# A state-space scan and two MLPs on one core: another order of the units and spread decays in the opening

## Chip, cores, metric

The kernel runs on one core of a Trainium2 chip. The metric is the device time of one execution in microseconds; lower is better. Before the change it is 644.33 us, the median of three runs (644.09 to 645.01).

## What is computed

Four batches of eight heads, 768 positions, head size 32, state size 16. A scan with decays `a` gives y, its 3072 rows of 256 go through an MLP with an ELU (256 to 2048 to 256) and then through a gated one (256 to 1536 to 256).

```python
for c in range(nc):                          # chunks of a sequence
    cum = cumsum(log(clip(a, 1e-6, 1))[c])
    L = exp(cum[i] - cum[j]) * (i >= j)
    y = ((C @ B.T) * L) @ x + (C @ state) * exp(cum)
    state = exp(sum(la)) * state + sum_j B[j] * x[j] * exp(cum[-1] - cum[j])
h = x @ w_in
x = where(h > 0, h, exp(min(h, 0)) - 1) @ w_out
out = (silu(x @ w_gate) * (x @ w_val)) @ w_out2
```

## The kernel before

The scan is cut into 24 units of 128 positions of one batch (all heads at once). Unit t belongs to batch t // 6, chunk t % 6, so four consecutive units mostly follow each other in one sequence. The first eight units (`CUT`) are handled as two halves of 64 positions (`R`) each. The tokens go through MLP 1 in six blocks of 512, four units a block.

Steps of a unit: E (L316), a scan on VectorE that turns the decays, broadcast by DMA to all partitions (`abc`), into the products of decays; P (L334), the running products per head (from `ahn`); cb (L375, TensorE) is B times C; m (L381) multiplies E by cb; bn and ct (L354, L346, GpSimd) weight B by the last column of E and C by P; u (L392, TensorE) is the unit's contribution to the state; sc (L403, L405, VectorE) steps the state; sb (L417, GpSimd) spreads it into block-diagonal form for y (L451 for the part from the state, L458 for the inner part); out (L474, ScalarE) and xl (L478, VectorE) split y into high and low parts xh and xl, the input of MLP 1. Later units do the same with other shapes (L442, L446, L370, L340). The state lies in two buffers `sc` that units use in turn: a unit reads one and writes the other.

MLP 1 runs in slots, one hidden tile f of 128 a slot: h (L493, six matmuls), ScalarE's relu and exp (L515, L520), VectorE's L521, c (L535 in block 0, L542 later). h has two PSUM banks, so h(i+2) waits for L521 of slot i. Weights come packed; tile f is decoded by ScalarE (ex, L137) and three steps on VectorE (L140, L143, L147), then split by ScalarE (wh, L179) and GpSimd (wl, L183). In block 0 each slot decodes the weight of three slots later, with the steps of units 4 to 7 among it.

Before the slots stands the opening: units 0 to 3 and the first weights. Every engine runs its instructions in the order in which they are written, and for the opening that order is written out by hand in `ORDER`, one word a step: `Labc0` loads abc of unit 0, `cl` clips it, `d10 d00 d20` are the decode steps of weight 0, `acl aclip acs` load all of `a`, clip it and write it to DRAM (`ac`), from where all units but the first two read their decays. `first.close()` then gives the PSUM banks of `cb_odd` and `y_odd` to h and c. All loads are issued by SyncE's queue (SP) in that same order. After the opening, `OFF`, `OFF1`, `OFF8` give for each step of a unit the slot and the place in it (early, mid, late).

Of the kernel before, what the change touches and what calls it, by code (L numbers as in the profile page):

```python
# [18 lines left out]
Q = 128  # L19
R = 64  # L20
# [38 lines left out]
ORDER = """Labc0 Lbc0 ident cl0 mz0 ident8 Labc1 cb0 Lahn0 LW0 E0 Lbc1 cl1 mz1 Lx0 Lahn1 ex0 d10 d00 P0 acl d20 E1 cb1 Lx1 blk
bn0 m0 wh0 Lbc2 aclip LW1 ct0 u0 wl0 acs P1 bn1 m1 sc0 sb0 ct1 ex1 u1 d01 y0 d11 Labc2 out0  # L60
LW2 Lahn2 xl0 Lx2 sc1 d21 sb1 wh1 y1 Labc3 wl1 mz2 E2 Lbc3 cb2 P2 out1 Lx3 bn2 xl1 Lahn3 ex2 ct2 m2 u2 LW3 d02 d12 d22 sc2 sb2
wh2 mz3 E3 cb3 y2 wl2 P3 bn3 out2 xl2 ct3 m3 u3 Labc4 Lbc4 Lx4 Lahn4 sc3 sb3 y3 out3 xl3 Labc5 Lbc5 Lx5 Lahn5""".split()

# [6 lines left out]
def ssm_mlp_glu_kernel(ctx, tc, a, bcs, xbc, w1, w2, consts, out):  # L70
# [41 lines left out]
    sbd = [ast.tile([128, 2, 128], F32, name=f"sbd{i}") for i in range(2)]  # L112
    sc = [ast.tile([128, 2, 2 * D], F32, name=f"sc{i}") for i in range(2)]

    ctz = [x2_all[:, 2 * NT - 2 * Q * (i + 1):2 * NT - 2 * Q * i].rearrange("p (g q) -> p g q", g=2) for i in range(2)]
    ident8_r = x2_all[:, 2 * NT - 4 * Q - H * R:2 * NT - 4 * Q]
    top = 2 * NT - 4 * Q - H * R - NT // 16

# [69 lines left out]
    an = BATCH * H * S // 128  # L188
    spare, at = {}, [0, 0]
    for t, tag, n in [(1, "bcraw", 1024), (2, "bcraw", 1024), (3, "bcraw", 1024), (1, "abc", 512), (2, "abc", 512),  # L190
                      (3, "abc", 512), (1, "xb", 512), (2, "xb", 512), (3, "xb", 512), (2, "E", 512),
                      (1, "ahn", 128), (2, "ahn", 128), (3, "ahn", 128)]:
        k = int(at[0] + n > top)
        spare[t, tag] = (x2_all, w2e)[k][:, at[k]:at[k] + n]
        at[k] += n

    for t, tag, i in [(5, "bcraw", 0), (6, "bcraw", 512), (7, "abc", 0), (4, "abc", 0)]:
        k = {5: 1, 6: 1, 7: 1, 4: 2}[t]
        spare[t, "xb"] = spare[k, tag][:, i:i + 512]
    acl = x2_all[:, top:top + an]  # L200
# [20 lines left out]
    def a_loads(t):  # L221
        b, c = divmod(t, NCH)
        u = U.setdefault(t, {})
# [96 lines left out]
    def q0(t):  # L320

        return 0 if t % NCH > 0 else R if t < CUT else Q

    def a_P(t):
        u = U[t]
        if q0(t) == Q:
            return
        z = u["ahn"][:, q0(t):]
        if t < DIRECT:
            nc.vector.tensor_scalar(z, z, 1.0, 1e-6, ALU.min, ALU.max)  # L330
        u["P"] = ap_.tile([128, Q], F32, tag="P", name="P")
# [89 lines left out]

    def a_sb(t):
        if t < CUT:
            spread(t, q0(t) // R, 2)
        if t + 1 >= CUT and t % NCH < NCH - 1:
            spread(t + 1, 0, 1)

    def a_state(t):
        a_sc(t)
        a_sb(t)  # L430
        if t >= CUT:
            U.pop(t)

    def a_y(t):


        u = U[t]
        has = t % NCH > 0
        if t >= CUT:
# [393 lines left out]
```

## Time and profile before

| | us |
|---|---|
| median of three runs | 644.33 |
| the profiled execution | 643.67 |
| its span, first to last instruction | 641.9 |
| TensorE busy | 616.2 |
| VectorE busy | 384.2 |
| ScalarE, GpSimd busy | 314.5, 315.5 |

The span is what the trace covers; the execution's own time is 1.8 us more. The engines run beside each other, so the busy times add up to far more than the span. In the rows below, a time that stands first is counted from the span's start.

### The profile page before, as it was taken

The page shows a single profiled execution, that of the slowest core. Times are in us where ns is not written, and L with a number is a line of the kernel's source. Part 1 is how long each engine was busy: PE and PEld are TensorE (multiplying, and loading weights), DVE is VectorE, ACT ScalarE, POOL GpSimd, SP SyncE. Part 2 cuts the span into 40 slices and gives each one's busy share as a digit, 9 for nine tenths or more (in the row PEclk, how much of TensorE's full clock was granted, in tenths as well). Part 3 has the DMA queues.
Part 4 walks back from the last instruction along what each step waited for, and adds up shares of the span by engine and source line. Part 5 has one row for each costly group of instructions (what it writes and reads, how often), then busy time and mean ns, then how long its engine had stood idle before and what let it go on. Part 6 is the DMA issues. An engine that isn't in the chain of part 4 may idle for free.

```text
span 641.9 us, 9664 instructions
## 1 busy us (share of the span) xinstructions
PE 616.2 (96%) x3620; PEld 490.1 (76%) x3620; DVE 384.2 (60%) x574; ACT 314.5 (49%) x568; POOL 315.5 (49%) x263
## 2 busy tenths in 40 slices
PE   2599999999999999999999999999999999999997
PEld 1456667888788878888888888888888888888886
DVE  5869987878887898783574663343343343343332
ACT  2156767667667766766775542322332232332322
POOL 3636756767878587874454333333333333333332
PEclk9999999999999999999999999999999999999999
DMA  6785534443543544400310000000000000000000
GB/s 184 203 287 193 168 117 145 138 146 128 144 143 132 152 133 132 135 34 18 98 51 0 2 2 0 34 0 1 33 1 1 33 1 0 34 0 2 33 1 33
DMA packets 21646, 49.54 MB, mean 77 GB/s; under 512 B 4320, under 2 KB 6496, under 8 KB 21600
## 3 DMA queue, kind: packets, MB, share of 16 engines
q1 hardware_dynamic: 21600, 48.93, 24.4%
q8 instruction: 28, 0.46, 0.3%
q14 instruction: 18, 0.15, 0.1%
HBM read 45.68 MB, written 3.24 MB: 76 GB/s over the span
## 4 chain that ended last, share of the span: by engine, by line
PE 94%; DVE 3%; issue 1%; SPq 1%; DMA 1%; ACT 0%; POOL 0%; POOLq 0%; DVEq 0%
PE h L493 21%; PE c L542 17%; PE o L493 15%; PE v L493 15%; PE g L493 15%; PE c L535 4%; PE cb L370 1%; PE y L446 1%; PE y L442 1%; DMA raw<-in_w 1%; DVE P L334 1%; DVE E L316 0%; DVE v L147 0%; PE y L392 0%; PE y L451 0%
## 5 line engine op out<-in xcount | busy, mean ns | idle before, releaser
L499 POOL TENSOR_TENSOR gl<-m,gh 128x512 fp32r<-128x512 f32 x152 | 200.2, 1320 | 249.1 <-ACT gh L498 244.0
L614 DVE TENSOR_TENSOR m<-m,g 128x512 f32<-128x512 f32 x72 | 49.5, 688 | 163.9 <-ACT m L609 163.9
L609 ACT ACTIVATE m<-g 128x512 f32<-128x512 f32 x72 | 43.0, 598 | 185.6 <-PE g L493 185.5
L521 DVE SCALAR_TENSOR_TENSOR m<-m,h 128x512 f32<-128x512 f32 x96 | 65.5, 682 | 59.2 <-ACT m L520 59.2
L498 ACT ACTIVATE gh<-m 128x512 fp32r<-128x512 f32 x152 | 94.8, 624 | 1.6 <-DVE m L615 1.0
L515 ACT ACTIVATE m<-h 128x512 f32<-128x512 f32 x96 | 56.8, 592 | 63.3 <-PE h L493 55.9
L493 PE MATMUL h<-xh,w1h 128*128 128x512 f32 x192 | 80.2, 418 | 1.6 <-DVE xl L478 1.1
L493 PE MATMUL h<-xh,w1l 128*128 128x512 f32 x192 | 75.6, 393 | 0.0
L542 PE MATMUL c<-gh,w1h 128*128 128x512 f32 x160 | 62.4, 390 | 0.0
L542 PE MATMUL c<-gh,w1l 128*128 128x512 f32 x160 | 62.3, 389 | 0.0
L520 ACT ACTIVATE m<-m 128x512 f32<-128x512 f32 x96 | 59.9, 624 | 0.5
L493 PE MATMUL h<-xl,w1h 128*128 128x512 f32 x192 | 59.8, 393 | 0.0
L493 PE MATMUL g<-x2h,w2h 128*128 128x512 f32 x144 | 56.0, 389 | 0.0
L493 PE MATMUL g<-x2h,w2l 128*128 128x512 f32 x144 | 56.0, 389 | 0.0
L493 PE MATMUL v<-x2h,w2h 128*128 128x512 f32 x144 | 56.0, 389 | 0.0
L493 PE MATMUL v<-x2h,w2l 128*128 128x512 f32 x144 | 56.0, 389 | 0.0
L493 PE MATMUL o<-gh,w2h 128*128 128x512 f32 x144 | 56.0, 389 | 0.0
L493 PE MATMUL o<-gh,w2l 128*128 128x512 f32 x144 | 56.0, 389 | 0.0
L493 PE MATMUL o<-gl,w2h 128*128 128x512 f32 x144 | 56.0, 389 | 0.0
L615 DVE TENSOR_TENSOR m<-m,v 128x512 f32<-128x512 f32 x72 | 49.5, 688 | 7.5
L542 PE MATMUL c<-gl,w1h 128*128 128x512 f32 x160 | 50.9, 389 | 0.0
L493 PEld LDWEIGHTS h<-xh,w1h 128*128 128x128 f32 x192 | 36.4, 189 | 14.0 <-DVE m L521 4.0
(125 smaller groups left out, 1089.4 us busy)
## 6 DMA issues: line engine op xcount, KB each, us to landing
abc<-ac SPq DMA_DIRECT2D x16, 512.0 KB
bcraw<-in_bcs SPq DMA_DIRECT2D x32, 256.0 KB
raw<-in_w SPq DMA_DIRECT2D x15, 512.0 KB
w2e<-in_w SPq DMA_DIRECT2D x12, 512.0 KB
xb<-in_xbc SPq DMA_DIRECT2D x17, 256.0 KB
raw<-in_w SPq DMA_DIRECT2D x12, 256.0 KB
out_y<-yo SPq DMA_DIRECT2D x12, 256.0 KB
abc<-ac SPq DMA_DIRECT2D x8, 128.0 KB
```

What stands on the lines that cost most here:

```text
L334: nc.vector.tensor_tensor_scan(u["P"][:, q:q + n], u["ahn"][:, q:q + n], zero_q[:, :n], 1.0, ALU.mult, ALU.add)
L493: nc.tensor.matmul(dst, lhsT=l, rhs=r, start=first and i == 0, stop=last and i == len(ops) - 1, **kw)
L498: nc.scalar.activation(hi, src, AF.Copy)
L499: lo_eng.tensor_tensor(lo, src, hi.bitcast(F32), ALU.subtract)
L515: nc.scalar.activation(m, h, AF.Relu, scale=-1.0)
L520: nc.scalar.activation(m, m, AF.Exp, scale=-1.0)
L521: nc.vector.scalar_tensor_tensor(m, m, -1.0, h, ALU.add, ALU.max)
L535: nc.tensor.matmul(cps[b][m], lhsT=W1["v", f][:, m * 128:(m + 1) * 128], rhs=g, start=f == 0, stop=f == NF1 - 1)
L542: nc.tensor.matmul(cps[b][m], lhsT=w[:, m * 128:(m + 1) * 128], rhs=r, start=f == 0 and w is wh and r is gh, stop=f == NF1 - 1 and r is gl)
L609: nc.scalar.activation(m, pg, AF.Sigmoid)
L614: nc.vector.tensor_tensor(m, m, pg, ALU.mult)
L615: nc.vector.tensor_tensor(m, m, pv, ALU.mult)
```

## The change

Units are numbered chunk by chunk over the batches: unit t belongs to batch t % 4, chunk t // 4. The first four units are then the first chunks of the four batches, and none of them has a state to start from; every later unit has one, which the unit four before it left. There are four state buffers, one for a batch, each updated in place: sc writes the half step into the second slice, sb spreads, and a new step sn writes the end state over the first slice. For units from 8 on the spread moves from the state step into the scan step of the unit that reads it. The last four units leave out u and the state.

The decays of units 0 to 3 come as one small tile on 8 partitions (`a8`), are clipped there, and TensorE spreads them over 128 partitions with a 0/1 matrix `sel`: two matmuls of 256 columns a unit (`ba`) into unused columns of the y banks, and one of 130 columns for each pair of units (`bp`) into unused columns of cb. The scan E reads them there in two halves; P of two units is one scan of 130 columns. A copy `el` of the last column of E on ScalarE serves bn. `sel`, `ident` and `blk` are loaded from ScalarE's queue. `ORDER` is rewritten; the decode of weight 2 stands after the last xl in it, and the loads of weights 4 and 5 move into it. For later units `lo` and `pe1` move within the slot.

```diff
-OFF1 = dict(OFF, hi=(-2, "l"), lo=(-1, "m"), pe1=(0, "l"), u=(4, "l"), state=(5, "e"))
+OFF1 = dict(OFF, hi=(-2, "l"), lo=(-1, "e"), pe1=(0, "m"), u=(4, "l"), state=(5, "e"))
...
+ORDER = """La0 sel La1 ident blk Lbc0 Lbc1 ident8 Lx0 cl0 cl1 ba0 bp0 cb0 ba1 bp1 E0 el0 E1 el1 Lx1 Lbc2 Lbc3 Lx2 Lx3 Lacl LW0 m0 P0 bn0 ct0 cb1 ba2 u0 m1 bn1 ct1 ba3 u1
+LW1 sc0 sb0 sn0 E2 el2 sc1 sb1 sn1 E3 el3 cb2 LW2 y0 cb3 out0 P1 m2 bn2 ct2 u2 y1 out1 m3 bn3 ct3 u3 xl0 aclip acs sc2 sb2 xl1 sc3 sb3 ex0 d10 d00 d20 y2 out2 wh0 y3 out3 wl0 sn2 sn3 xl2
+ex1 d11 d01 d21 xl3 wh1 wl1 ex2 d12 d02 d22 wh2 wl2 
+LW3 Labc4 Lbc4 Lahn4 Lx4 LW4 LW5""".split()
...
+    def a0_spread(t):
+        y = U[t]["y"] = (y_ps, y_odd)[t % 2]
+        U[t]["ab"] = y[:, :, 4 * R:]
+        for k in range(2):
+            nc.tensor.matmul(U[t]["ab"][:, k], lhsT=sel[:, Q * t:Q * t + Q], rhs=a8s[:, 4 * R * k:4 * R * k + 4 * R], start=True, stop=True)
+
+    def a0_spread_p(j):
+        n = R + 1
+        nc.tensor.matmul(cb_ps[:, j, 4 * R:4 * R + 2 * n], lhsT=sel[:, H * R:], rhs=a8[:, H * R + 2 * n * j:H * R + 2 * n * j + 2 * n],
+                         start=True, stop=True)
+
+    def a0_E(t):
+        e = U[t]["E"] = U[t]["buf"]([128, H, R], "E")
+        for k in range(2):
+            hs = slice(4 * k, 4 * k + 4)
+            nc.vector.tensor_tensor_scan(e[:, hs].rearrange("p h q -> p (h q)"), U[t]["ab"][:, k],
+                                         ident8_r[:, 4 * R * k:4 * R * k + 4 * R], 0.0, ALU.mult, ALU.add)
...
     def a_scan(t):
+        if t >= CUT:
+            a_sb(t)
         for z in (a_prep, a_P, a_E, a_ct, a_bn):
...
-        s, y, nxt = sc[t % 2], u["y"], sc[(t + 1) % 2][:, 0]
-        c = t % NCH
+        s, y = sc[t % BATCH], u["y"]
+        nxt = s[:, 0]
...
+    def a_sn(t):
+        s = sc[t % BATCH]
+        nc.vector.scalar_tensor_tensor(s[:, 0], s[:, 1], U[t]["P"][:, Q - 1:Q], U[t]["y"][:, 1, :2 * D], ALU.mult, ALU.add)
...
     def a_state(t):
         a_sc(t)
-        a_sb(t)
-        if t >= CUT:
+        if t < CUT:
+            a_sb(t)
+            a_sn(t)
+        else:
             U.pop(t)
...
-            if f >= 4:
-                at(mid, max(-2, f - nw - LEAD), load_w1, f)
+            if f >= 6:
+                at(mid, max(-1, f - nw - LEAD), load_w1, f)
+        at(mid, -1, a_load, n0 + 1)
+        at(mid, -1, a_load_x, n0 + 1)
```

## Rows read from the trace of the kernel before

**Rows 1.** The page, part 1: busy us (share of the span) and instructions of each engine.

```profile
PE 616.2 (96%) x3620; PEld 490.1 (76%) x3620; DVE 384.2 (60%) x574; ACT 314.5 (49%) x568; POOL 315.5 (49%) x263
```

**Rows 2.** Stretches: us, busy us (instructions) by engine, clock, DMA share, GB/s.

```profile
0.00:34.60 34.60, 13.82 (x334) 10.31 (x334) 22.59 (x47) 7.71 (x13) 14.92 (x25) 1.00 0.67 195
...
38.90:86.20 47.30, 46.22 (x446) 28.05 (x446) 45.92 (x78) 31.30 (x56) 30.31 (x29) 1.00 0.63 206
...
86.20:350.00 263.80, 263.80 (x1590) 210.25 (x1568) 197.56 (x288) 180.05 (x338) 178.34 (x138) 1.00 0.35 108
```

**Rows 3.** The chain of waits, in order of time: start us, us, what.

```profile
34.18 0.43 DVE xl L478
...
34.66 2.94 PE h L493 x6
...
45.70 1.72 PE c L535 x4
...
111.32 0.42 PE y L442 x4
```

**Rows 4.** Timeline of VectorE, opening: start us, us, line, operation, out, in.

```profile
6.42 1.23 DVE L316 TENSOR_TENSOR_SCAN E<-abc,x 128x512 f32<-128x512 f32 x1 [1.23 <-ACT x L648]
...
19.52 1.18 DVE L147 SCALAR_TENSOR_TENSOR v<-e,v 128x512 uint32<-128x512 uint32 x1
...
26.54 1.57 DVE L316 TENSOR_TENSOR_SCAN E<-x 128x512 f32<-128x512 f32 x1
...
29.61 0.39 DVE L478 TENSOR_TENSOR xl<-y,xh 128x256 fp32r<-128x256 f32 x1
...
29.93 0.67 DVE L381 TENSOR_TENSOR E<-E,cbo 128x512 f32<-128x512 f32 x1
...
34.52 0.45 DVE L140 TENSOR_SCALAR v<-raw 128x512 uint16<-128x512 uint16 x1
...
34.86 0.45 DVE L143 TENSOR_SCALAR v<-raw 128x512 uint16<-128x512 uint16 x1
```

**Rows 5.** Timeline of TensorE, opening, and one row of block 0.

```profile
11.86 0.47 PE L392 MATMUL y<-xb 64*32 64x64 f32 x16 [0.57 <-POOL xb L354]
...
20.21 1.22 PE L451 MATMUL yo<-x,sbd 128*128 128x128 f32 x4 [2.06 <-POOL sbd L417]
...
21.97 1.13 PE L375 MATMUL cb<-x 16*64 16x64 f32 x32
...
38.97 0.69 PE L375 MATMUL cb<-bcraw 16*64 16x64 f32 x32
```

**Rows 6.** Timelines of SyncE's queue, ScalarE and VectorE: loads and their first readers.

```profile
3.07 0.42 SPq L647 DMA_DIRECT2D con<-in_consts  x1
...
5.75 0.63 ACT L648 ACTIVATE x<-con 128x512 f32<-128x512 f32 x1 [3.74 <-DMA con<-in_consts]
...
5.46 0.41 SPq L131 DMA_DIRECT2D raw<-in_w  x1
...
9.76 0.46 DVE L143 TENSOR_SCALAR v<-raw 128x512 uint16<-128x512 uint16 x1 [1.66 <-DMA raw<-in_w]
```

**Rows 7.** Timeline of VectorE, block 0.

```profile
38.92 0.69 DVE L521 SCALAR_TENSOR_TENSOR m<-m,h 128x512 f32<-128x512 f32 x1 [2.40 <-ACT m L520]
...
47.89 0.59 DVE L405 SCALAR_TENSOR_TENSOR sc<-sc,P,y 128x64 f32<-128x64 f32 x2
...
48.40 0.75 DVE L140 TENSOR_SCALAR v<-w2e 128x512 uint16<-128x512 uint16 x1
...
49.04 0.97 DVE L143 TENSOR_SCALAR v<-w2e 128x512 uint16<-128x512 uint16 x1
```

**Rows 8.** Timeline of GpSimd, opening and block 0.

```profile
26.99 2.19 POOL L183 TENSOR_TENSOR w1l<-v,w1h 128x512 fp32r<-128x512 f32 x1
...
30.93 0.72 POOL L417 TENSOR_TENSOR sbd<-sc,con 128x256 f32<-128x256 f32 x1
...
47.52 1.30 POOL L183 TENSOR_TENSOR w1l<-v,w1h 128x512 fp32r<-128x512 f32 x1 [1.86 <-ACT w1h L179]
```

More of the change, by code (lines that the diff above doesn't have):

```diff
@@ L55 @@
 PWS = 2
-DIRECT = 2
 W2K = [0,0,1,2]
 W2N = 2
[L59 to L62, printed above, removed]
+ORDER = """La0 sel La1 ident blk Lbc0 Lbc1 ident8 Lx0 cl0 cl1 ba0 bp0 cb0 ba1 bp1 E0 el0 E1 el1 Lx1 Lbc2 Lbc3 Lx2 Lx3 Lacl LW0 m0 P0 bn0 ct0 cb1 ba2 u0 m1 bn1 ct1 ba3 u1
+LW1 sc0 sb0 sn0 E2 el2 sc1 sb1 sn1 E3 el3 cb2 LW2 y0 cb3 out0 P1 m2 bn2 ct2 u2 y1 out1 m3 bn3 ct3 u3 xl0 aclip acs sc2 sb2 xl1 sc3 sb3 ex0 d10 d00 d20 y2 out2 wh0 y3 out3 wl0 sn2 sn3 xl2
+ex1 d11 d01 d21 xl3 wh1 wl1 ex2 d12 d02 d22 wh2 wl2
+LW3 Labc4 Lbc4 Lahn4 Lx4 LW4 LW5""".split()
 REBIAS = 2.0 ** -112
@@ L112, in ssm_mlp_glu_kernel @@
     sbd = [ast.tile([128, 2, 128], F32, name=f"sbd{i}") for i in range(2)]
-    sc = [ast.tile([128, 2, 2 * D], F32, name=f"sc{i}") for i in range(2)]
     ctz = [x2_all[:, 2 * NT - 2 * Q * (i + 1):2 * NT - 2 * Q * i].rearrange("p (g q) -> p g q", g=2) for i in range(2)]
-    ident8_r = x2_all[:, 2 * NT - 4 * Q - H * R:2 * NT - 4 * Q]
-    top = 2 * NT - 4 * Q - H * R - NT // 16
+    low = 2 * NT - 4 * Q - 4 * D * BATCH
+    sc = [x2_all[:, low + 4 * D * i:low + 4 * D * i + 4 * D].rearrange("p (s q) -> p s q", s=2) for i in range(BATCH)]
+    ident8_r = x2_all[:, low - H * R:low]
+    top = low - H * R - NT // 16
     def decode(src, raw=None):
@@ L188, in ssm_mlp_glu_kernel @@
     an = BATCH * H * S // 128
[L189 to L199, printed above, removed]
+    spare = {}
+    for k, t, tag, i, n in [(0, 1, "bcraw", 0, 1024), (0, 2, "bcraw", 1024, 1024), (0, 3, "bcraw", 2048, 1024), (0, 5, "xb", 0, 512),
[3 rows of a table added]
+                            (1, 2, "xb", 5120, 512), (1, 3, "xb", 5632, 512)] + [(0, t, "el", 4096 + H * t, H) for t in range(4)]:
+        spare[t, tag] = (x2_all, w2e)[k][:, i:i + n]
+    sel, one, a8 = spare[0, "sel"][:H], spare[0, "one"], spare[0, "as"][:H]
+    a8s, a8p = a8[:, :H * R], a8[:, H * R:].rearrange("h (t r) -> h t r", t=BATCH)
     acl = x2_all[:, top:top + an]
@@ L237, in a_loads @@
         u["buf"] = buf
-        src = a if t < DIRECT else ac
+        src = ac
         def bc():
@@ L280, in ahn @@
                     nc.sync.dma_start(u["ahn"][:, R * k:R * k + R], bass.AP(s.tensor, s.offset, [[R, H], [0, N], [1, R]]))
-        return dict(abc=abc, bc=bc, x=xb, ahn=ahn)
+        return dict(bc=bc, x=xb) if t < BATCH else dict(abc=abc, bc=bc, x=xb, ahn=ahn)
     def a_load(t):
@@ L304, in a_lo, with a0_load, a0_clip, a0_P @@
                 eng.tensor_tensor(u[z], u[raw], u[z].bitcast(F32), ALU.subtract)
-    def a_cl(t):
-        nc.vector.tensor_scalar(U[t]["abc"], U[t]["abc"], 1.0, 1e-6, ALU.min, ALU.max)
+    def a0_load(p):
+        if p:
+            nc.sync.dma_start(a8p[:, :, 1:], bass.AP(a.tensor, a.offset + H * R, [[R, H], [H * Q, BATCH], [1, R]]))
+        else:
+            nc.sync.dma_start(a8s, bass.AP(a.tensor, a.offset, [[H * R, H], [1, H * R]]))
+    def a0_clip(p):
+        z = a8p[:, :, 1:] if p else a8s
+        nc.vector.tensor_scalar(z, z, 1.0, 1e-6, ALU.min, ALU.max)
+        if not p:
+            nc.vector.memset(a8s.rearrange("h (g r) -> h g r", r=R)[:, :, 0:1], 0.0)
+    def a0_spread(t):
[13 more added lines that the diff above has]
+                                         ident8_r[:, 4 * R * k:4 * R * k + 4 * R], 0.0, ALU.mult, ALU.add)
+    def a0_P(j):
+        n = R + 1
+        nc.vector.tensor_tensor_scan(spare[j, "P"][:, R:], cb_ps[:, j, 4 * R:4 * R + 2 * n], one, 0.0, ALU.mult, ALU.add)
+        for i in range(2):
+            U[2 * j + i]["P"] = spare[j, "P"][:, n * i + 1:n * i + 1 + Q]
     def a_prep(t):
@@ L349, in a_bn @@
         u = U[t]
-        if t >= CUT and t % NCH == NCH - 1:
+        if t >= CUT and t >= NU - BATCH:
             return
@@ L389, in a_u @@
             ks = slice(D * k, D * k + D)
-            for s in range(2 if t % NCH < NCH - 1 else 1) if t < CUT else range(t % NCH < NCH - 1):
+            for s in range(2 if t < NU - BATCH else 1) if t < CUT else range(t < NU - BATCH):
                 rs = slice(R * s, R * s + R) if t < CUT else slice(0, Q)
@@ L418, in spread @@
             sbd[t % 2][:, k:n].rearrange("p s (i q) -> p s i q", i=2),
-            sc[t % 2][:, k:n].unsqueeze(2).to_broadcast([128, n - k, 2, 2 * D]),
+            sc[t % BATCH][:, k:n].unsqueeze(2).to_broadcast([128, n - k, 2, 2 * D]),
             blk_sb.rearrange("p (i q) -> p i q", i=2).unsqueeze(1).to_broadcast([128, n - k, 2, 2 * D]), ALU.mult)
     def a_sb(t):
[L423 to L426, printed above, removed]
+        spread(t, *((q0(t) // R, 2) if t < CUT else (0, 1)))
     def a_state(t):
         a_sc(t)
-        a_sb(t)
-        if t >= CUT:
+        if t < CUT:
+            a_sb(t)
+            a_sn(t)
+        else:
             U.pop(t)
@@ L437, in a_y @@
         u = U[t]
-        has = t % NCH > 0
+        has = t >= BATCH
         if t >= CUT:
@@ L642, in ssm_mlp_glu_kernel @@
         nc.vector.memset(zero_q, 0.0)
+        nc.gpsimd.memset(a8p[:, :, 0:1], 0.0)
+        nc.gpsimd.memset(one, 0.0)
+        nc.gpsimd.memset(one.rearrange("p (t r) -> p t r", t=2)[:, :, 0:1], 1.0)
         for z in ctz:
@@ L646, in ssm_mlp_glu_kernel @@
         tok = {
-            "ident": lambda: nc.sync.dma_start(ident_r, consts[:, :R]),
+            "ident": lambda: nc.scalar.dma_start(ident_r, consts[:, :R]),
             "ident8": lambda: nc.scalar.activation(ident8_r.rearrange("p (h q) -> p h q", h=H), ident_r.unsqueeze(1).to_broadcast([128, H, R]), AF.Copy),
-            "blk": lambda: nc.sync.dma_start(con[:, R:R + 2 * Q + 2], consts[:, R:]),
-            "acl": a_clip0, "aclip": a_clip, "acs": a_clip1,
+            "sel": lambda: nc.scalar.dma_start(sel, consts[:H, R + 2 * Q + 2:]),
+            "blk": lambda: nc.scalar.dma_start(con[:, R:R + 2 * Q + 2], consts[:, R:R + 2 * Q + 2]),
+            "Lacl": a_clip0, "aclip": a_clip, "acs": a_clip1,
         }
@@ L654, in ssm_mlp_glu_kernel @@
                 tok[f"L{nm}{t}"] = lambda t=t, nm=nm: a_loads(t)[nm]()
+            if t < 2:
+                for nm, fn in dict(La=a0_load, cl=a0_clip, bp=a0_spread_p, P=a0_P).items():
+                    tok[f"{nm}{t}"] = lambda t=t, fn=fn: fn(t)
             if t < n0:
-                for nm, fn in dict(cl=a_cl, mz=a_prep, E=a_E, P=a_P, ct=a_ct, bn=a_bn, cb=a_pe1, m=a_m, u=a_u, sc=a_sc,
-                                   sb=a_sb, y=a_y, out=a_out, xl=a_xl).items():
+                for nm, fn in dict(ba=a0_spread, el=a_el, E=a0_E, ct=a_ct, bn=a_bn, cb=a_pe1, m=a_m, u=a_u, sc=a_sc,
+                                   sb=a_sb, sn=a_sn, y=a_y, out=a_out, xl=a_xl).items():
                     tok[f"{nm}{t}"] = lambda t=t, fn=fn: fn(t)
-        for f in range(4):
+        for f in range(6):
             tok[f"LW{f}"] = lambda f=f: load_w1(f)
@@ L815 @@
         con[p, R + Q + p // N % 4 * D:R + Q + (p // N % 4 + 1) * D] = 1.0
-        con[p, -2:] = p // N % 4 >= 2, p // N % 2
+        con[p, R + 2 * Q:R + 2 * Q + 2] = p // N % 4 >= 2, p // N % 2
+        con[p // N, R + 2 * Q + 2 + H * R + p] = 1.0
+    for p in range(H * R):
+        con[p // R, R + 2 * Q + 2 + p] = 1.0
     arrays = {
```

36 lines of the change are left out of this document (19 added, 17 removed), and 3 rows, old and new, of the table spare.

## The prediction

> **What bounds the kernel now.** I read the page first: TensorE (PE) is busy 96% of the span [rows 1], so on the whole PE sets the time, and only a stretch in which it is not full can give much. The table of stretches shows which [rows 2]: up to 34.6 us PE works 13.8 us while VectorE (DVE) works 22.6; from 38.9 to 86.2 us, while block 0 of the first MLP runs beside the decoding of its weights, PE has 46.2 of 47.3 us and DVE 45.9, so the two are level; from 86.2 us on PE is simply full. The chain of waits puts the turning point at 34.66 us [rows 3]: the first h matmul starts there, released by the subtraction xl of unit 3 (its PSUM banks are those of the opening). What brings that matmul forward brings the end forward, unless block 0 gives it back. In block 0 the point to watch is L521, the last read of h(i): h(i+2) takes its bank. The first one is at 38.92 us [rows 7], and from there DVE has next to no idle time up to 86 us, so any instruction that DVE must wait for there moves PE.
>
> **The opening, before.** It is a chain along one sequence: four consecutive units of one batch, so each unit's state needs the last one's, and DVE's in-order queue carries clips, 512-column scans, P scans over two broadcast tiles, and three weight decodes (W0 to W2) ahead of the last xl. Many of these ops are long: a scan E takes 1.23 us at 6.42 and 1.57 at 26.54, the second half of a decode 1.18 [rows 4].
>
> **What it removes.** The four broadcast tiles abc and the ahn tiles (DMA), their clips (now on 8 partitions), the state passed between units 0 to 3, and W2's decode, which moves behind the last xl. The DRAM copy of a (acs) no longer stands ahead of units 2 and 3, only of unit 4.
>
> **What it adds, on PE.** The spreads ba are two fp32 matmuls of 256 columns per unit, four instructions. Four of 512 columns take 1.72 us in block 0 [rows 3]. In the opening PE runs at half of that: the same 32 cb matmuls take 1.13 us at 21.97 and 0.69 at 38.97 [rows 5], so 1.2 against 2.4 GHz, although the table's clock column says 1.00 [rows 2]. Four of 256 columns at 1.2 GHz then cost the same 1.7 us. bp (130 columns) is 0.43 likewise. So PE does ba0 bp0 cb0 ba1 bp1 cb1 ba2 u0 ba3 u1 in 4 x 1.7 + 2 x 0.43 + 2 x 1.13 + 2 x 0.4 (u: 0.47 from idle [rows 5]) = 10.7 us. Its start: the small loads of a and sel are first on two queues; the con load was issued at 3.07 and used at 5.75, 2.3 us after its issue ended [rows 6], so a lands at about 3.5, the clip takes 0.4, and PE starts at about 4.0 and is through at 14.8.
>
> **The opening, after.** Up to 14.8 us PE leads; DVE's E0, E1, m0, P0, m1, sc0, E2 fit between. Then PE needs cb2 (1.13), y0 (about 1.0) and cb3 (1.13), 18.1; m3 follows, 0.6 a step [rows 4], 18.7. From there DVE leads in its own order: xl0 0.35, clip 0.2, sc2 0.2, xl1 0.35 with 0.35 of waiting for y1 and its copy, sc3 0.2: 20.35. Then W0's decode, sn2 and sn3 (0.5), xl2 (0.35), W1's decode, xl3 (0.35). A decode alone steps 0.35 + 0.35 + 0.6 = 1.3; beside GpSimd (POOL) work the last step took 1.18 [rows 4] and the first two stepped 0.64 and 1.07 [rows 7], up to 2.9 in all. sb3 and wl0 do run beside, so I take 1.95 and 2.4. **The first h then starts at 26.0 us** instead of 34.66. Both decodes at 1.3 give about 24.2; both at 2.9, with E2 and E3 at 1.57, give about 28.
>
> For the scans I take 1.2 (two halves) and not 1.57: the latter ran beside a wl on POOL (26.99 [rows 8]), and in the new order no wl comes before the scans are over. The Trainium skill, "SBUF — State Buffer", section Who interferes with whom, says that a DVE instruction with two SBUF inputs contends with a POOL instruction that reads SBUF, and one with a single SBUF input doesn't; the new scans read PSUM and one SBUF tile. By the rule the 1.57 of the trace can't occur there; without it, 0.4 us for each of E2 and E3 comes on top, which is inside the 28 above.
>
> **From the first h to the first L521.** W2's decode and W3's now stand between, and so do their wh on ScalarE, ahead of the relu of h0. h0 takes 2.94 us [rows 3], so L521 could follow as before after 4.26 us (38.92 less 34.66), but two decodes of 2.1 and the ScalarE copies make it about 4.8: 30.8. That is **8.1 us earlier**. Raw W3 must wait for W0's decode (its buffer) and is issued at 22.4, behind acs; W0 was there 3.9 us after its issue ended [rows 6], so W3 is at 26.7 for a use at 28: close, but hidden. Unit 4's loads queue behind it, issued up to 26 us and used from 31.
>
> **Units 4 to 7, the new wait.** The state of a batch is now one buffer, updated in place. sn (the second half step) writes the slice that sb on POOL still has to read, so DVE waits for sb. sb stands on POOL behind wl of a weight. In all four units wl starts 0.37 us ahead of sc (47.52 against 47.89 [rows 7, 8]). So sb can start 0.93 us after sc does, and takes 0.72 alone [rows 8]: sn starts 1.7 us after sc instead of 0.26, 1.4 us of waiting, with the next decode step and everything after it queued behind. On the other side, those two decode steps, now 0.64 and 1.07 a step beside sb [rows 7], would run after sb at 0.35 and 0.45. Net 0.5 us for unit 4, as much for 5 (which gains a second step) and 7, some 0.7 for 6, which also gets a full P: **2.4 us in all**. Bounds: 1.5 (the rest of the decode faster too) and 6.0 (4 x 1.4 + 0.4, nothing won back). As L521 has no slack here, I take it to move PE one for one.
>
> **Later blocks.** Units 12 and 18 have a state now and get four L442 matmuls each, 0.42 us [rows 3], where PE is full: **0.8 us**, less 0.1 for one u fewer. lo an entry earlier, pe1 and the spread at another place in the slot: nothing, since PE stays full while DVE has 66 us of idle time in these 264 us [rows 2]; if cover is gone, one spread of 0.72 for each of 16 units, at most 11 us, which I think unlikely as the spread is wanted four slots later.
>
> **Sum.** The profiled run took 643.67 us for a span of 641.9, and 0.66 less than the median of 644.33. 643.67 - 8.1 + 2.4 + 0.7 = 638.7; with the 0.66, **639.3 us**. Its own range, from the first h at 24.2 to 28 and the wait at 1.5 to 3.5: 636.5 to 642.5.
>
> **Rivals.**
> *The clock rises in the opening.* PE now works almost without a gap from 4 to 14.8 us. Against it: from 20.21 to 23.1 us PE also ran with hardly a gap, and the cb matmuls at its end were still slow [rows 5]; even h0's six matmuls of 512 columns ran at the low clock, 2.94 us [rows 3]. For it: the new stretch is more than three times as long. If the clock is at 2.4 GHz from about 9 us, cb1, ba2, ba3 and what follows cost half, DVE leads from 10 us on, the first h comes at about 23, and its own 2.94 us become some 1.5: some 3.5 us more, 635.8. The Trainium skill, "TensorE: Matmul & The Clock Gate", Part 1, has it that sustained matmul activity releases the throttle; by that rule the rival would be the forecast, but the stretch from 20.21 us, after which the clock was still low, doesn't bear it out.
>
> *The wait in the state costs its gross price*: 6.0 instead of 2.4, 642.9.
>
> *The in-place state eats it all.* Same place, but with wl as slow as the 2.19 us at 26.99 [rows 8] and no decode step won back: 2.3 us per unit and 0.4 for the added steps, 9.6 in all; 8.1 - 9.6 - 0.7 is a loss of 2.2, 646.5. It turns slower from 1.85 us per unit on. Against it: the wl there was slowed by scans and decodes on DVE, which would be waiting.
>
> *The opening isn't shorter than by 3 us*, since PE and DVE take turns (ba2 needs E0, u0 needs bn0, E2 stands behind sc0) and small loads come late: 644.3.
>
> **How the numbers follow.** Forecast 0.50, clock 0.27, gross wait 0.09, eaten 0.06, opening hardly shorter 0.08. The range for 8 in 10 reaches from 635.3 to 643.0: it leaves out the last two and the fast end of the clock's case. Of the gross wait part lies within 0.2% of before (which is about what a measurement can tell from no change): faster 0.84, same 0.09, slower 0.07.
>
> **What would show it.** In the trace after: the first h between 24 and 28 us (22 to 24, with cb matmuls near 0.7 us before it, if the clock rose); L521 first at about 31; in units 4 to 7 sn about 1.7 us after sc, released by POOL, and the decode steps behind it near 0.35 and 0.45; L442 in two more units. I am wrong if PE waits in block 0 for DVE by more than 1 us per unit, or if raw weights land later than their decodes want them.

## The result, and the profile after

The changed kernel takes **638.73 us** (median of 4 runs, 638.64 to 638.76) against 644.31 beside it: a ratio of 0.9911, 95% interval 0.9894 to 0.9929. The forecast was 639.3. Its profiled execution took 638.73 us, its span is 637.0 (641.9 before).

The page, part 1, and three stretches to set beside [rows 1, 2]: up to the new first h, in block 0 from the ELU product (L561) of slot 2 to that of slot 12, and in the later blocks (us, busy us and instructions by engine, clock, DMA share, GB/s):

```profile
PE 622.2 (98%) x3644; PEld 494.3 (78%) x3644; DVE 360.2 (57%) x571; ACT 316.5 (50%) x572; POOL 313.8 (49%) x269
...
0.00:27.86 27.86, 20.23 (x348) 14.45 (x349) 15.74 (x38) 6.38 (x14) 8.10 (x26) 1.00 0.50 163
40.34:81.86 41.52, 39.01 (x359) 23.83 (x357) 34.96 (x69) 26.09 (x46) 24.09 (x23) 1.00 0.68 213
82.00:345.00 263.00, 262.50 (x1590) 209.44 (x1582) 181.15 (x290) 182.00 (x337) 181.67 (x142) 1.00 0.35 109
```

The opening is 6.8 us shorter though TensorE does 6.4 us more in it; VectorE does 6.9 us less. Block 0 is less full. Between the same two products the kernel before has:

```profile
46.69:85.52 38.83, 38.22 (x345) 23.15 (x344) 37.68 (x67) 26.13 (x46) 24.94 (x24) 1.00 0.58 184
```

So TensorE is idle there for 2.51 us, where it was 0.61, and busy 0.8 us longer.

Where the 4.9 us of span came from is read off the same instruction in both timelines. L521 is L561 now, the h matmuls L533; a block ends where ScalarE reads c (`x<-c`).

| | before | after | lead of after |
|---|---|---|---|
| first h | 34.66 | 27.86 | 6.80 |
| first ELU product (slot 0) | 38.92 | 32.57 | 6.35 |
| the same, slot 2 | 46.69 | 40.34 | 6.35 |
| the same, slot 12 | 85.52 | 81.86 | 3.66 |
| block 0 ends | 99.68 | 95.92 | 3.76 |
| block 1 | 154.41 | 150.65 | 3.76 |
| block 2 | 205.49 | 201.26 | 4.23 |
| block 3 | 256.21 | 251.76 | 4.45 |
| block 4 | 304.81 | 300.08 | 4.73 |
| span | 641.9 | 637.0 | 4.9 |

So three terms: the opening -6.35 (forecast -8.1), block 0 +2.6 (forecast +2.4), the later blocks -1.1 (forecast +0.7). The total was near because the first and the last miss cancel.

**The opening, after.** TensorE's timeline (start us, us, line, operation, out, in, tile, count; in brackets the idle time before and what ended it), to set beside [rows 5]:

```profile
3.37 2.07 PE L321 MATMUL y<-w2e 8*128 8x256 f32 x4 [3.37 <-DVE w2e L314]
...
5.80 1.13 PE L414 MATMUL cb<-bcraw 16*64 16x64 f32 x32
...
14.75 0.47 PE L431 MATMUL yo<-w2e 64*32 64x64 f32 x16
...
17.54 1.13 PE L414 MATMUL cbo<-x 16*64 16x64 f32 x32
18.59 0.47 PE L431 MATMUL y<-w2e 64*32 64x64 f32 x16
...
20.98 0.47 PE L431 MATMUL yo<-w2e 64*32 64x64 f32 x16 [0.59 <-POOL x L376]
...
27.86 0.77 PE L533 MATMUL h<-xh,w1h 128*128 128x512 f32 x1 [3.58 <-DVE xl L518]
...
32.73 0.69 PE L414 MATMUL cb<-bcraw 16*64 16x64 f32 x32
```

The first row is ba of unit 0, the spread of its decays. TensorE then has no gap that matters up to 18.6 us and leads, and cb still takes 1.13 us at 17.54, the price at 1.2 GHz; 0.69 comes only at 32.73. VectorE's timeline, beside [rows 4]:

```profile
13.38 1.26 DVE L332 TENSOR_TENSOR_SCAN w2e<-y,x 128x256 f32<-128x256 f32 x2
...
18.80 0.69 DVE L420 TENSOR_TENSOR w2e<-w2e,cbo 128x512 f32<-128x512 f32 x1 [0.86 <-PE cbo L414]
...
21.61 0.42 DVE L518 TENSOR_TENSOR xl<-yo,xh 128x256 fp32r<-128x256 f32 x1 [1.49 <-PE yo L431]
...
24.90 0.28 DVE L454 SCALAR_TENSOR_TENSOR x<-x,w2e,yo 128x64 f32<-128x64 f32 x1 [0.78 <-ACT xh L514]
...
27.30 0.42 DVE L518 TENSOR_TENSOR xl<-yo,xh 128x256 fp32r<-128x256 f32 x1
...
32.57 0.67 DVE L561 SCALAR_TENSOR_TENSOR m<-m,h 128x512 f32<-128x512 f32 x1
```

ScalarE's copy of y1 (out1):

```profile
20.50 0.38 ACT L514 ACTIVATE xh<-yo 128x256 fp32r<-128x256 f32 x1 [2.40 <-PE yo L498]
```

From m3 at 18.80 VectorE leads, as forecast, but it waits longer than the sum had it. The PSUM tile `yo` (two banks) holds y of a unit and, in other columns, its u. xl1 (21.61) stands 1.49 us. Some 0.8 of them are for a result that it needs: y1 and its copy out1, which ends at 20.88. The other 0.7 are for u3, which TensorE writes into other columns of `yo` and which starts only at 20.98, behind out1; the row names GpSimd's L376 for that, but this had ended by 20.52. sn3 (24.90) stands 0.78 us for ScalarE, whose out3 only reads that tile. This last wait fits what the Trainium skill, "PSUM — Partial Sum Buffer", section PSUM bank collisions raise a hardware error, says: two engines' accesses to one bank have to be kept apart by waits, two reads too.

**Block 0, after.** VectorE and GpSimd around the state step of unit 4, beside [rows 7, 8], and the row of VectorE's waits (us in total, times, longest):

```profile
41.53 0.27 DVE L444 SCALAR_TENSOR_TENSOR x<-x,P,y 128x64 f32<-128x64 f32 x1
43.19 0.28 DVE L454 SCALAR_TENSOR_TENSOR x<-x,P,y 128x64 f32<-128x64 f32 x1 [1.39 <-POOL sbd L458]
43.39 0.45 DVE L140 TENSOR_SCALAR v<-w2e 128x512 uint16<-128x512 uint16 x1
43.73 0.45 DVE L143 TENSOR_SCALAR v<-w2e 128x512 uint16<-128x512 uint16 x1
```

```profile
41.16 1.30 POOL L183 TENSOR_TENSOR w1l<-v,w1h 128x512 fp32r<-128x512 f32 x1 [1.85 <-ACT w1h L179]
42.41 0.74 POOL L458 TENSOR_TENSOR sbd<-x,con 128x256 f32<-128x256 f32 x1
```

```profile
DVE x L454 <- POOL sbd L458: 5.5, 4, 1.4
```

This is the forecast wait to the tenth: sc at 41.53, sn 1.66 us later, behind sb, which stands behind wl on GpSimd; the two decode steps after it then take 0.45 us each instead of 0.75 and 0.97. On TensorE the time is lost ahead of u of units 5 to 7, 0.89, 0.81 and 0.81 us (0.37, nothing and 0.23 before). The profile names no releaser there, but VectorE's timeline has one, xl of the unit before:

```profile
49.58 0.41 DVE L518 TENSOR_TENSOR xl<-y,xh 128x256 fp32r<-128x256 f32 x1
```

```profile
50.09 0.35 PE L431 MATMUL y<-x 64*32 64x64 f32 x16 [0.89 <-issue]
```

xl reads y of unit 4 out of the PSUM tile into which u of unit 5 goes, in other columns. Each u of these units that TensorE waited for, here and before, starts 0.10 us after that xl ends. So VectorE's delay seems to reach TensorE through the shared y tile; no run took that sharing away.

**Later blocks, after.** The chain of waits where a unit of blocks 1 to 4 passes (start us, us, what):

```profile
120.57 0.60 PE cb L409 x7
121.17 0.27 PE y L482 x4
121.44 0.57 PE y L486 x16
122.01 0.11 PE y L431 x8
```

The y matmuls from the state (L442 before, L482 now) hold the chain for 0.27 us, not 0.42 [rows 3]. They now stand behind cb, whose tiles are 64x128 like theirs; before they stood behind c, whose tiles are 128x128, as the row ahead of that of [rows 3] shows:

```profile
109.96 1.36 PE c L542 x6
```

### The profile page after: what moved, and what is told of

It reads as the page before. It is cut to its first block, busy times and chain, and to the rows that moved or that the text cites. A ratio compares the mean times of both kernels' runs of the same rounds, so it can differ in the third digit from the quotient of the medians.

```text
span 637.0 us, 9691 instructions
## 1 busy us (share of the span) xinstructions
PE 622.2 (98%) x3644; PEld 494.3 (78%) x3644; DVE 360.2 (57%) x571; ACT 316.5 (50%) x572; POOL 313.8 (49%) x269
## 4 chain that ended last, share of the span: by engine, by line
PE 85%; DVE 3%; POOL 0%; issue 0%; ACT 0%; DMA 0%; SPq 0%; DVEq 0%
PE h L533 17%; PE c L582 16%; PE o L533 15%; PE v L533 15%; PE g L533 15%; PE cb L409 2%; PE y L486 1%; PE c L575 1%; PE y L482 1%; DVE E L348 1%; DVE v L143 0%; DVE v L147 0%; DVE m L561 0%; DVE v L140 0%; DVE zc L302 0%
## 5 line engine op out<-in xcount | busy, mean ns | idle before, releaser
L539 POOL TENSOR_TENSOR gl<-m,gh 128x512 fp32r<-128x512 f32 x152 | 203.4, 1339 | 259.4 <-ACT gh L538 256.2
L561 DVE SCALAR_TENSOR_TENSOR m<-m,h 128x512 f32<-128x512 f32 x96 | 65.6, 683 | 65.4 <-ACT m L560 65.2
L533 PE MATMUL h<-xh,w1h 128*128 128x512 f32 x192 | 80.6, 420 | 4.2 <-DVE xl L518 3.6
L533 PE MATMUL h<-xh,w1l 128*128 128x512 f32 x192 | 76.1, 396 | 0.0
L533 PE MATMUL h<-xl,w1h 128*128 128x512 f32 x192 | 59.7, 393 | 0.0
L533 PE MATMUL v<-x2h,w2h 128*128 128x512 f32 x144 | 56.0, 389 | 0.0
L533 PE MATMUL g<-x2h,w2h 128*128 128x512 f32 x144 | 56.0, 389 | 0.0
L533 PE MATMUL o<-gh,w2h 128*128 128x512 f32 x144 | 56.0, 389 | 0.0
L533 PE MATMUL o<-gh,w2l 128*128 128x512 f32 x144 | 56.0, 389 | 0.0
L533 PE MATMUL o<-gl,w2h 128*128 128x512 f32 x144 | 56.0, 389 | 0.0
L533 PE MATMUL v<-x2h,w2l 128*128 128x512 f32 x144 | 56.0, 389 | 0.0
L533 PE MATMUL g<-x2h,w2l 128*128 128x512 f32 x144 | 56.0, 389 | 0.0
L533 PEld LDWEIGHTS h<-xh,w1h 128*128 128x128 f32 x192 | 36.5, 190 | 17.4 <-DVE m L561 4.9
```

The source lines that it names most:

```text
L533: nc.tensor.matmul(dst, lhsT=l, rhs=r, start=first and i == 0, stop=last and i == len(ops) - 1, **kw)
L539: lo_eng.tensor_tensor(lo, src, hi.bitcast(F32), ALU.subtract)
L561: nc.vector.scalar_tensor_tensor(m, m, -1.0, h, ALU.add, ALU.max)
```

## Experiments: who leads the opening

**TensorE first.** The spreads are issued twice:

```diff
-        for k in range(2):
+        for k in (0, 0, 1, 1):
```

> The changed kernel with each of the spread matmuls ba issued twice (the same result), 1.7 us more on TensorE per unit. Theory A (TensorE leads the opening until u of unit 1, as predicted): u1 comes 6.8 us later, the first h at about 34 and the time at 644 to 645.5. Theory B (VectorE's own work leads): at most 2 us more, 640.7.

645.73 us (645.20 to 646.67), ratio 1.0021 (1.0011 to 1.0030): slower than before the change. TensorE's timeline:

```profile
3.49 3.78 PE L321 MATMUL y<-w2e 8*128 8x256 f32 x8 [3.49 <-DVE w2e L314]
...
34.81 0.76 PE L533 MATMUL h<-xh,w1h 128*128 128x512 f32 x1 [3.59 <-DVE xl L518]
```

Each spread got 1.7 us longer, 6.8 in all; the first h came 6.95 later and the time rose by 7.0. Up to the last spread, time added on TensorE is time of the kernel, one for one. The rival that the opening would be hardly shorter, since TensorE and VectorE take turns, fails: TensorE leads up to there, and 6.8 us were gained.

**Then VectorE's order.** The two waits of the timeline above are given other work: sn2 and sn3 go behind their sc, and the first two steps of W0's decode ahead of xl1 (the end of that line of `ORDER`).

```diff
-... xl0 aclip acs sc2 sb2 xl1 sc3 sb3 ex0 d10 d00 d20 y2 out2 wh0 y3 out3 wl0 sn2 sn3 xl2
+... xl0 aclip acs sc2 sb2 sn2 ex0 d10 d00 xl1 sc3 sb3 sn3 d20 y2 out2 wh0 y3 out3 wl0 xl2
```

> The changed kernel with another order of the opening's end: sn2 and sn3 right behind sc2 and sc3 instead of behind the copies of y2 and y3, and two decode steps of weight 0 ahead of xl of unit 1. Theory A: VectorE's waits of 1.5 us (ahead of xl of unit 1) and 0.8 us (ahead of sn3) are what made the opening longer than predicted; the first h starts at about 26.2 us instead of 27.86 and the time is about 637.1. Theory B: what stands between the first h and the first L561 (decodes of weights 2 and 3, and the landing of weight 3) sets block 0, and an earlier first h is worth at most 0.3 us: 638.4 or more.

637.21 us (637.15 to 637.59), ratio 0.9890 (0.9875 to 0.9905). VectorE:

```profile
20.50 0.48 DVE L143 TENSOR_SCALAR v<-raw 128x512 uint16<-128x512 uint16 x1
20.88 0.70 DVE L140 TENSOR_SCALAR v<-raw 128x512 uint16<-128x512 uint16 x1
21.75 0.42 DVE L518 TENSOR_TENSOR xl<-yo,xh 128x256 fp32r<-128x256 f32 x1 [0.18 <-PE yo L431]
```

The wait of xl1 is 0.18 us, that of sn3 gone; the first h is at 26.70 and the first ELU product at 31.41, both 1.16 us earlier than in the changed kernel. A new wait of 0.80 us (the decode of W1 for its ex on ScalarE) keeps the rest. So the two waits, not a slower piece of work, are most of what the first h came late by: 1.16 of 1.86 us came back.

**W2's decode.** The change put it behind the last xl; here it is ahead again.

```diff
-ex1 d11 d01 d21 xl3 wh1 wl1 ex2 d12 d02 d22 wh2 wl2
+ex1 d11 d01 d21 wh1 wl1 ex2 d12 d02 d22 xl3 wh2 wl2
```

> The changed kernel with weight 2's decode ahead of the last xl of the opening again, as before the change. Theory A: the first h starts 1.9 us later (29.8 us) and, as the first L561 follows the first h by at least the 4.3 us of the relu and exp chain, it comes at about 34.0 instead of 32.57: the time is 640.1. Theory B: VectorE has the same work ahead of the first L561 in either order, which alone counts: 638.7, whatever the first h does.

640.97 us (640.66 to 641.29), +2.2. The first h is at 30.82, and the first ELU product now waits for ScalarE (VectorE's timeline):

```profile
35.05 0.69 DVE L561 SCALAR_TENSOR_TENSOR m<-m,h 128x512 f32<-128x512 f32 x1 [2.02 <-ACT m L560]
```

The first h is 2.96 us later but only 2.48 of it reach the first product. That one part of the change is worth 2.2 us: work that h0 doesn't need runs beside h0. How the rest of the opening's 6.35 us divides between the new order of the units (no state passed among the first four) and the spread of the decays on TensorE, no run shows: none has one without the other.

## Experiments: the clock

**Wide work just before h.** Two fp32 matmuls of 128x512 follow y3; their result is used nowhere.

```diff
-... y3 out3 wl0 sn2 sn3 xl2
+... y3 wm out3 wl0 sn2 sn3 xl2
...
+            "wm": lambda: [nc.tensor.matmul(cb_ps[:, k], lhsT=ident, rhs=ident8_r, start=True, stop=True) for k in range(2)],
```

> The changed kernel with two fp32 matmuls of 128x128 by 512 columns more behind y of unit 3 (their result is used nowhere), in the 3.6 us in which TensorE waits for the last xl. Theory A: 21 us of nearly unbroken small matmuls left the clock at 1.2 GHz and full-width work raises it; h0 and h1 run at 2.4 GHz (1.4 us instead of 2.7 for six), but the first L561 is held by the decodes of weights 2 and 3, so the time is 638.2 to 638.7. Theory B: the clock goes by time alone, h0 is as slow as before, 638.7. Theory C: h0 at the higher clock brings the whole chain forward, 637.4.

638.60 us (638.53 to 638.67). TensorE:

```profile
24.07 3.78 PE L694 MATMUL cb<-x,con 128*128 128x512 f32 x4
...
28.24 0.39 PE L533 MATMUL h<-xh,w1l 128*128 128x512 f32 x1
...
33.17 0.50 PE L533 MATMUL h<-xh,w1h 128*128 128x512 f32 x1 [1.63 <-DVE abc L342]
```

The clock is at 2.4 GHz when h starts (0.39 us a matmul, 0.63 in the changed kernel), h0 and h1 are through 1.9 us sooner, and TensorE then waits 1.63 us for VectorE, whose first ELU product starts at 32.44 instead of 32.57. This is theory A: at this place the clock is worth nothing, VectorE leads.

**Wide work at the start.** Matmuls of ones, 4.2 us of them, run while the first loads are under way; their result is used nowhere either.

```diff
+        ones = ident8.rearrange("p h q -> p (h q)")[:, :512]
+        nc.vector.memset(ones, 1.0)
+        for n in (512, 512, 256):
+            nc.tensor.matmul(cb_odd[:, 0, :n], lhsT=ones[:, :Q], rhs=ones[:, :n], start=True, stop=True)
```

> The changed kernel with 4.3 us of full-width fp32 matmuls at the very start (512, 512 and 256 columns of ones, their result is used nowhere), so that the first spread starts some 2.3 us later. Theory A: they raise the clock and the small work that follows keeps it; the spreads take 0.85 us instead of 1.7 a unit, cb 0.6 instead of 1.1, and the first h comes 1.5 to 2.5 us earlier: 636.5 to 637.5. Theory B: the small work does not keep it or it never rises; everything of the opening is 2.3 us later, 641.0.

638.65 us (638.53 to 641.52), no gain. TensorE, and two stretches:

```profile
5.73 1.13 PE L321 MATMUL y<-w2e 8*128 8x256 f32 x4
...
9.11 1.13 PE L414 MATMUL cbo<-x 16*64 16x64 f32 x32
10.17 2.07 PE L321 MATMUL y<-w2e 8*128 8x256 f32 x4
```

```profile
5.00:10.00 5.00, 5.00 (x79) 3.84 (x77) 2.47 (x5) 0.22 (x1) 0.40 (x1) 0.86 0.88 288
10.00:30.00 20.00, 15.74 (x290) 10.83 (x283) 14.52 (x34) 5.09 (x13) 8.06 (x17) 0.50 0.48 157
```

The median is neither figure of the expectation. In the profiled run the wide matmuls did raise the clock: ba takes 1.13 us at 5.73, where it took 2.07. But from about 9 us on everything is slow again, though TensorE had no gap: the granted clock is 0.86 from 5 to 10 us and 0.50 after. Between 5.73 us and the fall it ran only ba, bp and cb. The 2.4 us of later start were just paid back (first h at 27.67): from ba0 to ba2 it takes 4.44 us instead of 6.99, and the first h follows one for one, now with time taken off TensorE. Three of the four runs have a mean granted clock of 0.981, like the profiled one; the fourth, at 641.52 us, has 0.999, like the changed kernel, and its time is that of theory B. What it did isn't shown; it would fit a run in which the clock didn't rise. So the clock rival fails, and for more than the forecast had: in the opening the clock didn't rise under its own matmuls, and when wide ones had raised it, it didn't stay up under them.

## Experiments: the wait in block 0

**sn two entries later**, behind the slot's ELU product:

```diff
-OFF = dict(..., state=(3, "e"), pe2=(4, "l"), out=(4, "l"), xl=(4, "l"))
+OFF = dict(..., state=(3, "e"), pe2=(4, "l"), out=(4, "l"), xl=(4, "l"), sn=(3, "l"))
...
-            a_sn(t)
...
```

> The changed kernel with sn of units 4 to 7 moved from just behind sb to the end of the same slot, so that VectorE's decode does not stand behind the wait for sb. Theory A (net price): the 1.4 us of waiting per unit go, but the two decode steps beside sb are slow again; units 4 to 7 together give back 2.0 to 2.7 us, 636.4. Theory B (gross price): 4 x 1.4 us, 633.1. Theory C (TensorE is the bound in block 0 and hides the wait): 638.7.

638.32 us (638.11 to 638.78): 0.4 less, nearest to theory C. VectorE's wait is gone and slot 12's product is 1.5 us earlier (80.35), but TensorE now waits, 0.82 us in unit 4 and 0.28 or 0.29 in the others, for y of each unit goes into a bank that sn reads:

```profile
45.30 0.71 PE L490 MATMUL y<-x,sbd 128*128 128x128 f32 x4 [0.82 <-DVE abc L342]
```

sn runs from 44.97 to 45.25; the row names the instruction beside it. TensorE reaches y of unit 7 at 81.28, as late as in the changed kernel (81.32), and block 0 ends only 0.29 us earlier (95.63): VectorE's gain is lost at that y.

**sn behind the three decode steps**, ahead of the product (a call of `a_sn` in the loop of the slots):

```diff
-            a_sn(t)
...
+            if f - nw in [FIRST[k] + 3 for k in range(4)]:
+                at(early, f - nw, a_sn, n0 + (f - nw) // 3 - 1)
```

> The changed kernel with sn of units 4 to 7 behind the three decode steps of the same slot, ahead of the slot's L561. At the end of the slot it came too late: y of the unit, on TensorE, had to wait 0.3 to 0.8 us for it. Theory A: neither VectorE nor TensorE waits now, block 0 is shorter by the net price of the wait, 1.5 us (what the last L561 of block 0 gained there), 637.2. Theory B: the wait costs TensorE nothing, as TensorE is as full as VectorE in block 0: 638.3 to 638.7. Theory C (gross price): 633.1.

637.69 us (637.60 to 637.96), -1.0, between theories A and B. From slot 2's product to slot 12's it takes 40.24 us; the changed kernel took 41.52, the one before 38.83. TensorE still waits for sn, 0.2 us a unit.

**Both orders together**, with ex1 ahead of wh0 on ScalarE as well, against the 0.80 us seen above (the lines of `ORDER` beside those of the reordered opening):

```diff
-... d20 y2 out2 wh0 y3 out3 wl0 xl2
-ex1 d11 d01 d21 xl3 wh1 wl1 ...
+... d20 y2 out2 ex1 wh0 y3 out3 wl0 xl2
+d11 d01 d21 xl3 wh1 wl1 ...
```

> The changed kernel with the opening's order of the earlier run (sn2, sn3 behind sc2, sc3; two decode steps of weight 0 ahead of xl of unit 1), ex of weight 1 ahead of the copies of weight 0 and of unit 3, and sn of units 4 to 7 behind the decode. Theory: the gains add up, 1.5 for the opening's order, 0.8 for VectorE's wait for ex of weight 1, 1.5 for the state: 634.9, the first h at about 25.9 us. Rival: once the state's wait is gone TensorE bounds block 0, and only the opening's part counts, 636.4.

636.57 us (636.50 to 636.91), ratio 0.9880 (0.9865 to 0.9895). The two gains nearly add up (1.5 and 1.0; together 2.2). The number alone would fit the rival's 636.4, but the trace doesn't: from the first product to the end of block 0 it takes 62.51 us, as much as with the move of sn alone (62.48), against 63.38 in the reordered opening alone, so the state's part counts in full. What fell short of the theory is ex1 above all. The move of ex1 brought h to 25.51, but the first product only to 31.31, 0.1 us: W2's decode then runs beside GpSimd's wl and its first two steps take 1.21 and 1.53 us.

**sn between the second and third decode step**, all else as in the last kernel:

```diff
-            at(early, f - nw, dec_w1, f)
+            unit = {FIRST[k] + 3: n0 + k for k in range(4)}.get(f - nw)
+            at(early, f - nw, dec_w1, f, (0, 1) if unit else (0, 1, 2))
+            if unit:
+                at(early, f - nw, a_sn, unit)
+                at(early, f - nw, dec_w1, f, (2,))
...
-            if f - nw in [FIRST[k] + 3 for k in range(4)]:
-                at(early, f - nw, a_sn, n0 + (f - nw) // 3 - 1)
```

> The kernel of e8_all_orders with one edit: in the first four units the sn of a unit is issued between the second and the third decode step, no longer behind all three. In e7_sn_after_decode TensorE's y of each of these units waited 0.2 us for sn. Theory A: TensorE's order bounds these units, so these four waits go, and the sum is 0.5 to 0.8 us less than e8's 636.57: 635.8 to 636.1 us. Theory B: VectorE bounds them; sn only changes places with one decode step and the time stays, 636.4 to 636.8 us.

**635.68 us** (635.38 to 636.38), ratio 0.9872 (0.9856 to 0.9889): the best version, 3.0 us under the changed kernel, a little better than theory A. VectorE and then TensorE:

```profile
40.62 1.07 DVE L140 TENSOR_SCALAR v<-w2e 128x512 uint16<-128x512 uint16 x1
41.58 0.97 DVE L143 TENSOR_SCALAR v<-w2e 128x512 uint16<-128x512 uint16 x1
42.45 0.26 DVE L454 SCALAR_TENSOR_TENSOR x<-x,P,y 128x64 f32<-128x64 f32 x1
```

```profile
43.18 0.61 PE L490 MATMUL y<-x,sbd 128*128 128x128 f32 x4
```

Neither engine waits at sn or at y. Slot 2 to slot 12 takes 39.46 us (39.23 to 78.69):

```profile
39.23:78.69 39.46, 38.46 (x355) 23.42 (x354) 38.84 (x68) 26.13 (x46) 24.84 (x23) 1.00 0.69 212
```

So of the 2.69 us that block 0 lost over this stretch in the changed kernel, 2.06 were the wait, 0.5 a unit, and 0.63 stay. Of these 0.39 are idle time of TensorE (1.00 us against 0.61 before), again ahead of u of units 5 to 7, which start 0.10 us past the end of xl, and 0.24 are work, as much as the two more matmuls take that y of unit 6 has now that it has a state (0.61 us against 0.38). The gain in time from the last two placements agrees: 1.04 and 0.89 are 1.9 us.

## Experiments: the later blocks

**The y behind c again.** Only the two places in the slot are put back:

```diff
-OFF1 = dict(OFF, hi=(-2, "l"), lo=(-1, "e"), pe1=(0, "m"), u=(4, "l"), state=(5, "e"))
+OFF1 = dict(OFF, hi=(-2, "l"), lo=(-1, "m"), pe1=(0, "l"), u=(4, "l"), state=(5, "e"))
```

> The changed kernel with lo and pe1 of the later units back at their old places in the slot, so that cb of the next unit comes behind y and u again instead of ahead of them. Theory A: the later blocks gained because the four state matmuls of y now follow cb, which has the same tile shape (64 rows by 128 columns), and TensorE changes shape once less per unit; then they take 0.42 us again instead of 0.27 in the chain of waits, 16 units lose 0.15 us each, and the time is 638.7 + 2.3 = 641.0. Theory B, that of the prediction: the place of cb costs and gains nothing, 638.7.

640.22 us (640.15 to 640.39), +1.5. The chain at the same unit:

```profile
118.74 1.36 PE c L582 x6
120.10 0.42 PE y L482 x4
120.52 0.57 PE y L486 x16
121.10 0.11 PE y L431 x8
121.21 0.59 PE cb L409 x7
```

The unit's other rows are as they were, y is 0.15 us longer. Blocks 2 and 3, of four units each, take 0.62 and 0.61 us more (four times 0.15), blocks 1 and 4 0.2 each. Without the two places the later blocks are thus 0.5 us longer than before the change (542.7 us from the end of block 0 to the end of the span, 542.2 before), close to the forecast 0.7.

**The same edit alone**, in the kernel before (its diff is the one above, the other way round):

> The kernel before with nothing but the places of lo and pe1 of the later units taken from the change. Theory A (one change of tile shape less per unit): the 14 units of 8 to 23 that have a state gain 0.15 us each, 644.3 - 2.1 = 642.2. Theory B (place costs nothing): 644.3.

643.16 us (642.70 to 644.00) against 644.32: ratio 0.9982 (0.9973 to 0.9992). Blocks 2, 3 and 4 are 0.59, 0.45 and 0.31 us shorter, block 1 is 0.35 longer: there cb, which now comes earlier, waits 0.6 us for VectorE's zc. So the place in the slot, which the forecast priced at nothing, is worth 1.2 to 1.5 us. That the shape of the neighbour's tiles makes the 0.15 us, and not something else that comes with the place, is a guess: no run varied the one without the other.

## Why the prediction was near, point by point

**The bound: right.** The opening was the stretch to shorten, and the spreads on TensorE lead it (the doubled spread).

**TensorE's 10.7 us from 4.0: near by two errors.** It started at 3.37, 0.6 us early, and ended u1 at 15.2, 0.4 us late, so the work took 11.9: a ba took 1.9 to 2.0 us a step instead of 1.7. The row of wide c matmuls that I halved and doubled has 1.72 in the chain of waits; in TensorE's timeline the same four take 1.88.

**The scans at 1.2: right.** 1.26 and 1.27, also for unit 2's, which starts at 13.38 while GpSimd's sb0 runs (13.29 to 13.74). The rule of the Trainium skill ("SBUF — State Buffer", Who interferes with whom) that a VectorE instruction with one SBUF input, outside the modes that use both ports, doesn't contend agrees with that; nothing like the 1.57 of [rows 4] came back. The test is weak: before the change a scan with two SBUF inputs took 1.23 us at 20.76 though a wl ran from 21.44. And the forecast told the rule without its exception: the decode steps have one input, too, and took 1.07 and 0.97 us beside GpSimd in the last kernel, 0.45 without.

**First h at 26.0: wrong by 1.9 us, inside its bounds.** The step that failed is the run through VectorE's order after m3, where waits were counted only for xl1, at 0.35. They were 1.49 (xl1) and 0.78 (sn3 for out3), 1.9 more; m3 was 0.7 late, and the decodes, at 1.76 and 1.87 instead of 1.95 and 2.4, took that back. Of the 1.9 some 0.4 are y1 and its copy, for which xl1 waited 0.8 instead of 0.35, and some 1.5 come from tiles shared in PSUM (0.7 for u3, 0.78 for out3). I had asked of each instruction which result it needs, not who else uses its PSUM bank. From h to the first product it was 4.71 us (forecast 4.8).

**The state's wait: right in place, size and price.** 1.66 us after sc (1.7), decode steps of 0.34 and 0.55 us to the next one (0.35 and 0.45), net 0.5 us a unit plus what units 5 and 6 have more: 2.6 against 2.4. The path was another: the forecast had TensorE wait at h for L521, but all 2.51 us of its idle time between slot 2 and slot 12 stand ahead of u, by the start times for VectorE's xl. The prices as the forecast lists them for the four units add up to 2.2, so its sum was 0.2 too high by its own terms. The rival that it costs its gross price, and the one that it eats all, fail: wl stayed at 1.30 (with its own 0.4 of added steps that rival would have turned slower from 1.75 us a unit on, not 1.85). Nor did a weight land too late: in the opening and in block 0 no engine waits for one.

**Later blocks: wrong sign.** The two more sets of y came, as said, and with the places put back the later blocks cost 0.5 us (forecast 0.7). The term that failed is "lo and pe1: nothing, since PE stays full": it gave back 1.2 to 1.5 us. A full engine hides no change in its own order; here the place of a group in TensorE's order changed what it costs.

**The clock: the rival failed.** TensorE was busy 20.2 of the first 27.9 us and stayed at 1.2 GHz: cb took 1.13 us at 17.54, and an h matmul 0.63 us, against 0.39 at 2.4 GHz. The Trainium skill, "TensorE: Matmul & The Clock Gate", Part 1, where sustained matmul activity releases the throttle, doesn't hold for these small matmuls as it stands; the trace decides.

## What to carry to other kernels

When an in-order queue is rewritten, go through each instruction twice: for the result that it needs, and for the PSUM bank that it shares with another engine; the second gave some 1.5 of the 1.9 us of waiting that this forecast lacked in the opening, and other work put into the waits brought the first h 1.16 us forward. An update in place can be nearly as cheap as a second buffer (here all but 0.4 to 0.6 us of block 0's loss came back) if the overwriting step stands just behind the last work that would have run slowly beside the reader: neither directly behind it (VectorE waits) nor later than the next writer of the bank needs it (TensorE waits). And a full engine's own order is worth a look: four small matmuls cost 0.15 us more a unit at one place than at another, 1.2 to 1.5 us in all.

## What was not expected of the hardware

- The opening's matmuls, without a gap from 3.4 to 18.6 us, left TensorE at 1.2 GHz (cb 1.13 us), and after wide ones had raised it to 2.4 (ba 1.13 us), it fell again at about 9 us with no gap on TensorE (granted clock 0.50).
- The column of the granted clock reads 1.00 in the changed kernel's opening although cb takes 1.13 us there. In the kernel with wide matmuls at the start, where the clock changes early, the same slow work reads 0.50. So the price of a known instruction tells the clock of an opening better than the column does.
- y from the state (four matmuls of 64x128) holds TensorE 0.27 us behind cb and 0.42 behind c; why is open.
